# Scaling attention values straight out of PSUM on VectorE in a fused attention and SwiGLU kernel

## The chip, the cores and the metric

The kernel runs on one core of a Trainium2 chip. A core has TensorE (PE in the profile, with its weight loads as PEld), VectorE (DVE), ScalarE (ACT), GpSimd (POOL) and SyncE (SP), which work on their own queues of instructions and wait for one another by semaphores. The metric is the device time of one execution in microseconds (us); lower is better.

## The reference

Attention with a local window of 96 keys and 8 global keys feeds a SwiGLU feed-forward block:

```python
# q, k, v: (4 batches, 8 heads, 768, 64) float32
scores = scale * np.matmul(q, k.transpose(0, 1, 3, 2)) + bias     # bias = -slope * distance
scores = np.where(is_global | is_local, scores, -1e9)
a = np.exp(scores - max)
a = a / (np.sum(a, axis=-1, keepdims=True) + 1e-09)
x = np.matmul(a, v)                  # to (3072 tokens, 512)
g = x @ w_gate                       # w_gate, w_val: (512, 1536)
out = (g * sigmoid(g) * (x @ w_val)) @ w_out                      # w_out: (1536, 512)
```

The kernel does the division last: it sums the unnormalized weights (the denominators, `den`) and the weighted values (the numerators, `num`), and multiplies `num` by the inverted `den`. Inputs are float32; the products are taken in float16 and summed in float32.

## The kernel before

The 3072 tokens are eight tiles of 384. A tile is half a batch (`half` 0 or 1). Attention is worked in pairs of heads (`Pair`) and quads of heads (`Quad`, two per batch, `g` 0 or 1). TensorE is kept busy by mixing attention steps of one batch into the feed-forward groups of the batch before.

PSUM has eight banks. Four, `a0` to `a3`, go round for the attention steps; three, `x0` to `x2`, go round for gate and value products; `o0` holds output sums:

```python
    state = {"tags": ["a0", "a1", "a2", "a3"], "n": 0, "x": ["x0", "x1", "x2"]}

    def bank(name, dt=FP32):
        tag = state["tags"][state["n"] % len(state["tags"])]
        state["n"] += 1
        return single(name, tag, dt)

    def banks(name, dt=FP32):
        return [bank(name, dt) for _ in range(2)]
```

A bank is written again only after the last reader of what it held before. A scores step takes two banks (one per head of the pair), a values step three. Work for the other engines can be put in the list `later`, from which one entry is issued ahead of each group of matmuls:

```python
    def run_later(n):
        for _ in range(n):
            if later:
                later.pop(0)()
    # class Quad (cut)
        def invert(self, den):
            dT = sb2.tile([128, TB], FP32, name="dT", tag="dT")
            self.dR = sb2.tile([128, TB // 32], FP32, name="dR", tag="dR")
            nc.vector.transpose(dT, den[:, 0:TB])
            nc.vector.reciprocal(
                out=self.dR, in_=dT.rearrange("p (n i) -> p n i", i=32)[:, :, 0])

        def spread(self):
            self.rb = sb2.tile([128, TB], FP32, name="rb", tag="rb")
            nc.vector.transpose(
                self.rb.rearrange("p (n i) -> p n i", i=32),
                self.dR.unsqueeze(2).broadcast_to([128, TB // 32, 32]))

        def values(self, half, bank, mul_eng):
            den = bank("den")
            self.weigh(half, den, None)
            srcs = []
            for side in range(2):
                num = bank("num")
                self.weigh(half, num, side)
                src = sb2.tile([128, TB], FP32, name="ns", tag="ns")
                nc.scalar.copy(out=src, in_=num[:, 0:TB])
                srcs.append(src)

            def scale_num(side):
                mul_eng.tensor_mul(self.x_out(half, side), srcs[side], self.rb)
            ... (cut: invert, spread and the products go into `later`)
```

`weigh` is the run of matmuls; `mul_eng` is VectorE for batch 0 and GpSimd for the others. With GpSimd, both products are issued together with `spread`; with VectorE they are two entries of their own. The feed-forward group takes tanh on ScalarE (`th`) and two operations on VectorE (`sl`, `hT`):

```python
    def gate_or_val(t, f, which, c0=0):
        products(t, f, which, c0, NC)          # four matmuls into one of x0, x1, x2
        dst = gv.pop((f, which))
        if which == 0:
            ...
            nc.scalar.activation(out=th, in_=dst[:, 0:TB], func=AF.Tanh, scale=0.5)
            nc.vector.scalar_tensor_tensor(
                out=sl, in0=th, scalar=1.0, in1=dst[:, 0:TB], op0=AluOp.add, op1=AluOp.mult)
            gv["sl"] = sl
        else:
            nc.vector.tensor_mul(hTs[t][:, f, :], dst[:, 0:TB], gv["sl"])
```

The attention steps come in lists, each inner list being one step of the loop below. `sc` and `sch` are scores, `va` is values (batch, g, half), `tr` and `trh` transposes, `fetch` transposes by DMA, `sp` puts `spread_keys` (three VectorE copies into `kT`, L407, L410, L411) into `later`:

```python
    def first(b):
        return [[tr(b, 0), tr(b, 1)],
                [sc(b, 0, 0), sc(b, 0, 1)], [sc(b, 1, 0), sc(b, 1, 1), fetch(b, 2, 3)],
                [sp(b, 2), va(b, 0, 0), sp(b, 3)],
                [sc(b, 2, 0), sc(b, 2, 1)],
                [sc(b, 3, 0), sc(b, 3, 1)], [va(b, 1, 0)]]

    def both(b):
        n = b + 1
        return [[sc(b, 0, 2), sc(b, 1, 2)], [sc(b, 2, 2), sc(b, 3, 2), fetch(n, 0, 1)],
                [va(b, 0, 1)], [sp(n, 0), va(b, 1, 1), sp(n, 1)],
                [sc(n, 0, 0), sc(n, 0, 1), fetch(n, 2, 3)], [sp(n, 2), sc(n, 1, 0), sc(n, 1, 1)],
                [va(n, 0, 0), sp(n, 3)], [sc(n, 2, 0), sc(n, 2, 1)],
                [sc(n, 3, 0), sc(n, 3, 1)], [va(n, 1, 0)]]

    half1 = [[trh(0)], [trh(1)], [sch(0, 0), sch(0, 1)], [trh(2)], [sch(1, 0), sch(1, 1)],
             [trh(3)], [va(0, 0, 1)], [sch(2, 0), sch(2, 1)],
             [sch(3, 0), sch(3, 1)], [va(0, 1, 1)]]
    stretches = [
        (ff(0, 0, 10), half1),
        (ff(0, 10, 12) + ff(1, 0, 3), []),
        (ff(1, 3, 12, (1, 1, 2)), fst),                      # fst = first(1)
        (ff(2, 0, 12, (1,)) + ff(3, 0, 12, (1,)), both(1)),
        (ff(4, 0, 12, (1,)) + ff(5, 0, 12, (1,)), both(2)),
        (ff(6, 0, 12, (1,)), second(3)),
        (ff(7, 0, 12, (1,)), [])]
    ... (cut)
        work = sum(g[0] for g in groups)
        quota = len(steps) / (work - (1.0, 0, 6.0, 6.0, 6.0, 6, 3.0)[n])
        owed = -0.1 if n == 0 else 0.4
        for w, t, f, which in groups:      # gate, val, and output parts where there are any
            ... (cut: loads; at a tile's first group all of `later` is issued)
            run_later(1)
            if which == 2:
                out_part(*outs.pop(0))
            else:
                gate_or_val(t, f, which, NC if t == 0 and f < 2 else 0)
            owed += w * quota
            while owed >= 1.0 and steps:
                run_later(len(later))
                for step in steps.pop(0):
                    step()
                owed -= 1.0
```

So a step that comes due first issues all that is still in `later`. Half 0 of batch 0 is done ahead of these loops by `denominators` and `numerators`, which multiply out of PSUM on VectorE.

Of the kernel before, what the change touches and what calls it, by code (L numbers as in the profile page):

```python
# [9 lines left out]
FP32 = mybir.dt.float32  # L10
# [27 lines left out]
def kernel(  # L38
# [12 lines left out]
    nc = tc.nc  # L51
# [13 lines left out]
    TB = 384  # L65
    scale = float(1.0 / np.sqrt(D))
# [24 lines left out]
    sb2 = ctx.enter_context(tc.tile_pool(name="sb2", bufs=2))  # L91
# [16 lines left out]
    for hp in range(2):  # L108
        for st, src in ((k32, k), (q32, q)):
            nc.sync.dma_start(  # L110
                out=st[:, 2 * hp:2 * hp + 2, :],
                in_=src[0, 2 * hp:2 * hp + 2, 0:TB, :].rearrange(
                    "h (p j) d -> p h (j d)", p=128))
# [29 lines left out]
    for j in range(J2):  # L143
        nc.vector.tensor_copy(
            out=perm[:, j, :, NG + j::J2],
            in_=identx.rearrange("p (c m) -> p c m", c=NC0))
        n = (NG - j + J2 - 1) // J2
        nc.vector.tensor_copy(
            out=perm[:, j, :, j:NG:J2],
            in_=identx[:, 0:n].unsqueeze(1).broadcast_to([128, NC0, n]))  # L150
# [85 lines left out]
# [4 lines that stand above are left out]
# [12 lines left out]
    later = []  # L252
# [163 lines left out]
    class Quad:  # L416
# [46 lines left out]
        def x_out(self, half, side):  # L463
            return x_of(2 * self.b + half)[:, 2 * self.g + side, :]

        def values(self, half, bank, mul_eng):
            den = bank("den")
            self.weigh(half, den, None)
            srcs = []
            for side in range(2):  # L470
                num = bank("num")
                self.weigh(half, num, side)
                src = sb2.tile([128, TB], FP32, name="ns", tag="ns")
                nc.scalar.copy(out=src, in_=num[:, 0:TB])  # L474
                srcs.append(src)

            def scale_num(side):
                mul_eng.tensor_mul(self.x_out(half, side), srcs[side], self.rb)  # L478

            def spread():  # L480
                self.spread()
                if mul_eng is nc.gpsimd:
                    for side in range(2):
                        scale_num(side)

            later.append(lambda: self.invert(den))
            later.append(spread)
            if mul_eng is not nc.gpsimd:
                for side in range(2):
                    later.append(lambda side=side: scale_num(side))  # L490

        def denominators(self, den):
            self.weigh(0, den, None)
# [2 lines left out]

        def numerators(self, side, num):
            self.weigh(0, num, side)
            nc.vector.tensor_mul(self.x_out(0, side), num[:, 0:TB], self.rb)


    hTs = {}
# [62 lines left out]
    quads = {(b, g): Quad(b, g) for b in range(B) for g in range(2)}  # L565
# [104 lines left out]
        return lambda: pairs[b, hp].scores(bk, nc.vector if on_vector else nc.gpsimd, bool(later))  # L670

    def va(b, g, half):
        return lambda: quads[b, g].values(half, bank, nc.vector if b == 0 else nc.gpsimd)

    def tr(b, hp):
        return pairs[b, hp].transposes
# [12 lines left out]
    def second(b):  # L689
        return [[sc(b, 0, 2), sc(b, 1, 2)], [sc(b, 2, 2), sc(b, 3, 2)],  # L690
                [va(b, 0, 1)], [va(b, 1, 1)]]
# [7 lines left out]
# [6 lines that stand above are left out]
# [131 lines left out]
```

The softmax here doesn't subtract the row's maximum and nothing guards it: scores larger than these inputs give would overflow.

## Time and profile before

| | |
|---|---|
| time, median of 3 | 253.78 us (253.47 to 254.28) |
| span of the profiled execution | 252.9 us |
| granted TensorE clock, mean | 0.998 |
| GpSimd products, L478 | 24, 23.9 us busy |
| ScalarE copies, L474 | 28, 12.0 us busy |
| tanh on ScalarE, L527 | 94, 46.4 us busy |
| VectorE sl, L529, and hT, L533 | 94 each, 51.8 and 51.7 us busy |

A group line of the profile names the source line, the engine, the operation, the output and inputs by the program's names, the shapes and the count, and then the busy time. A timeline line has start, length, engine, line and what it does; overlapping instructions of one kind are merged with a count (x2), so that two products of 0.55 us can show as one piece of 1.01. In brackets is the idle time before it on that engine, and what ended it. Busy times of one engine can overlap a little, and matmul ends are modelled.

### The profile page before, as it was taken

What the parts mean: (1) busy time and instruction counts of PE and PEld (TensorE: products, weight loads), DVE (VectorE), ACT (ScalarE), POOL (GpSimd) and SP (SyncE); (2) the same over time, 40 slices, a digit from 0 to 9 for tenths busy, and PEclk for the clock granted to TensorE, in tenths of its full rate; (3) what the DMA queues carried; (4) which work ended last, traced back from release to release, by engine and by line L of the source; (5) the groups of instructions that cost most, each with busy time, mean ns of one, the idle gap of its engine ahead of it and who ended that gap; (6) DMA issues with size and microseconds to landing.
All of it is one profiled execution on the core that took longest, in us unless ns stands there. A gap on an engine that the chain in (4) does not pass through costs nothing.

```text
span 252.9 us, 5999 instructions
## 1 busy us (share of the span) xinstructions
PE 241.3 (95%) x2384; PEld 136.1 (54%) x2384; DVE 168.7 (67%) x379; ACT 130.9 (52%) x290; POOL 105.0 (42%) x123
## 2 busy tenths in 40 slices
PE   6997999899889999999999999999999999999994
PEld 4664556464435556555555555555555555555541
DVE  7365779856695666979785656978875666555510
ACT  3476787559464455464653653555735634332321
POOL 9663664550054975913609865803020232200000
PEclk9999999999999999999999999999999999999999
DMA  6999999991950999993916997991011101100122
GB/s 157 188 203 181 180 207 205 167 131 42 127 69 4 141 150 173 129 143 64 117 44 67 150 157 88 147 109 45 0 44 41 44 0 44 43 20 24 41 83 83
DMA packets 86499, 25.63 MB, mean 101 GB/s; under 512 B 76288, under 2 KB 83528, under 8 KB 86472
## 3 DMA queue, kind: packets, MB, share of 16 engines
q0 software_dynamic: 65408, 13.83, 65.7%
q1 hardware_dynamic: 20920, 11.30, 21.8%
q8 instruction: 18, 0.29, 0.5%
q10 hardware_dynamic: 144, 0.13, 0.2%
q14 instruction: 9, 0.07, 0.1%
HBM read 28.63 MB, written 6.29 MB: 138 GB/s over the span
## 4 chain that ended last, share of the span: by engine, by line
PE 80%; DVE 8%; ACT 4%; DMA 3%; SPq 2%; issue 1%; DVEq 0%; ACTq 0%
PE ops L545 23%; PE gps L516 22%; PE vps L516 22%; PE num L443 3%; PE sc L366 2%; PE den L443 2%; DVE sl L529 2%; DMA kN<-kst 2%; DMA q<-in_q_dram 2%; ACT at L351 1%; PE trs L296 1%; PE warm L574 1%; PE sc L343 1%; PE psv L598 1%; SPq L399 1%
## 5 line engine op out<-in xcount | busy, mean ns | idle before, releaser
L529 DVE SCALAR_TENSOR_TENSOR sl<-th,gps 128x384 f32<-128x384 f32 x94 | 51.8, 552 | 45.4 <-ACT th L527 44.3
L527 ACT ACTIVATE th<-gps 128x384 f32<-128x384 f32 x94 | 46.4, 494 | 63.1 <-PE gps L516 61.6
L516 PE MATMUL gps<-xT,wg 128*128 128x384 f16 x376 | 77.0, 326 | 0.7 <-DVE xT L478 0.6
L516 PE MATMUL vps<-xT,wv 128*128 128x384 f16 x376 | 76.5, 326 | 0.5 <-DVE sl L529 0.4
L545 PE MATMUL ops<-wo,hT 128*128 128x512 f16 x288 | 75.5, 379 | 0.0
L533 DVE TENSOR_TENSOR hT<-vps,sl 128x384 f16<-128x384 f32 x94 | 51.7, 550 | 7.2
L478 POOL TENSOR_TENSOR xT<-ns,rb 128x384 f16<-128x384 f32 x24 | 23.9, 1013 | 77.5 <-DVE rb L459 62.4
L516 PEld LDWEIGHTS <-wg 128*128 128x128 f16 x384 | 35.8, 98 | 33.1 <-issue 3.1
L516 PEld LDWEIGHTS <-wv 128*128 128x128 f16 x384 | 36.8, 98 | 26.4 <-issue 2.1
L545 PEld LDWEIGHTS <-hT 128*128 128x128 f16 x288 | 27.4, 98 | 25.1 <-issue 0.4
L375 ACT ACTIVATE at<-sc 128x432 f16<-128x432 f32 x72 | 33.6, 535 | 9.0 <-PE sc L366 9.0
L171 POOL DMA_DIRECT2D vS<-in_v_dram x25 | 22.3, 898 | 9.1 <-DMA k<-in_k_dram 3.4
L559 ACT ACTIVATE osb<-ops 128x512 f32<-128x512 f32 x23 | 13.7, 597 | 18.0 <-PE ops L545 18.0
L474 ACT COPY ns<-num 128x384 f32<-128x384 f32 x28 | 12.0, 482 | 12.7 <-PE num L443 11.9
L203 POOL DMA_DIRECT2D qst<-in_q_dram x20 | 16.8, 854 | 2.7 <-DMA wo<-in_moe_w_out_dram 1.6
L203 POOL DMA_DIRECT2D kst<-in_k_dram x20 | 17.0, 865 | 2.0 <-DMA wo<-in_moe_w_out_dram 1.1
L386 DVE TENSOR_TENSOR at<-at,masks 128x864 f16<-128x864 f16 x20 | 12.9, 645 | 4.4 <-ACT at L375 4.4
L351 ACT ACTIVATE at<-sc 128x432 f16<-128x432 f32 (+2 forms) x32 | 11.5, 447 | 5.1 <-PE sc L343 5.1
L386 POOL TENSOR_TENSOR at<-at,masks 128x864 f16<-128x864 f16 x4 | 7.3, 1821 | 13.6 <-ACT at L375 13.6
L443 PE MATMUL num<-at,vS 128*32 128x216 f16 (+6 forms) x560 | 12.0, 226 | 0.0
L443 PE MATMUL den<-at,ones 128*32 128x216 f16 (+6 forms) x288 | 9.4, 229 | 2.4 <-DVE at L383 1.8
L443 PEld LDWEIGHTS <-ones 128*32 128x32 f16 x288 | 5.7, 96 | 9.2 <-issue 8.9
(76 smaller groups left out, 176.1 us busy)
## 6 DMA issues: line engine op xcount, KB each, us to landing
out_dram<-osb SPq DMA_DIRECT2D x23, 256.0 KB, 2.0
vS<-in_v_dram POOLq DMA_DIRECT2D x21, 120.0 KB, 8.1
kst<-in_k_dram POOLq DMA_DIRECT2D x20, 96.0 KB, 4.9
qst<-in_q_dram POOLq DMA_DIRECT2D x20, 96.0 KB, 4.7
wg<-in_moe_w_gate_dram POOLq DMA_DIRECT2D x6, 256.0 KB, 8.6
wv<-in_moe_w_val_dram POOLq DMA_DIRECT2D x6, 256.0 KB, 9.6
wo<-in_moe_w_out_dram POOLq DMA_DIRECT2D x3, 512.0 KB, 11.1
k<-in_k_dram SPq DMA_DIRECT2D x2, 192.0 KB, 3.8
```

The costliest lines, as they stand in the source:

```text
L171: nc.gpsimd.dma_start(out=vSs[b][NG:NG + n, c, :, :], in_=v[b, :, KC * c:KC * c + n, :].rearrange("h p d -> p h d"))
L203: nc.gpsimd.dma_start(out=rows_of(st, b, h // 2)[:, :, h % 2, :], in_=src[b, h].rearrange("(t p) d -> p t d", p=128))
L351: nc.scalar.activation(out=at[:, hi, 0:col + n], in_=sc[hi][:, 0:col + n], func=AF.Exp, scale=scale)
L375: nc.scalar.activation(out=at[:, hi, :], in_=sc[hi][:, 0:BANK], func=AF.Exp, scale=scale)
L386: mul_eng.tensor_mul(at, at, m[:, :, o:o + BANK])
L443: nc.tensor.matmul(dst[r, o:o + n], lhsT=ones[:, 0:32] if side is None else vals[:, 4 * g + j, side::2], rhs=pairs[b, 2 * g + j // 2].at[c ...
L478: mul_eng.tensor_mul(self.x_out(half, side), srcs[side], self.rb)
L516: nc.tensor.matmul(gv[f, which][:, 0:TB], lhsT=w[:, c, 128 * f:128 * f + 128], rhs=x_of(t)[:, c, :], start=(c == 0), stop=(c == NC - 1))
L527: nc.scalar.activation(out=th, in_=dst[:, 0:TB], func=AF.Tanh, scale=0.5)
L529: nc.vector.scalar_tensor_tensor(out=sl, in0=th, scalar=1.0, in1=dst[:, 0:TB], op0=AluOp.add, op1=AluOp.mult)
L533: nc.vector.tensor_mul(hTs[t][:, f, :], dst[:, 0:TB], gv["sl"])
L545: nc.tensor.matmul(ops, lhsT=hTs[t][:, f, 128 * i:128 * i + 128], rhs=wo[:, f, :], start=(f == 0), stop=(f == NFF - 1))
```

## The change

The values of all batches are multiplied by the inverted denominators on VectorE, reading the numerators out of PSUM. The copy to SBUF on ScalarE and the product on GpSimd go. The aim is to drop a step between the matmul and the finished values and to use one path for all batches; ScalarE and GpSimd have less to do, and the bank of a numerator is read by its product itself.

```diff
-        def values(self, half, bank, mul_eng):
+        def values(self, half, bank):
             den = bank("den")
             self.weigh(half, den, None)
-            srcs = []
+            later.append(lambda: self.invert(den))
+            later.append(self.spread)
             for side in range(2):
                 num = bank("num")
                 self.weigh(half, num, side)
-                src = sb2.tile([128, TB], FP32, name="ns", tag="ns")
-                nc.scalar.copy(out=src, in_=num[:, 0:TB])
-                srcs.append(src)
-
-            def scale_num(side):
-                mul_eng.tensor_mul(self.x_out(half, side), srcs[side], self.rb)
-
-            def spread():
-                self.spread()
-                if mul_eng is nc.gpsimd:
-                    for side in range(2):
-                        scale_num(side)
-
-            later.append(lambda: self.invert(den))
-            later.append(spread)
-            if mul_eng is not nc.gpsimd:
-                for side in range(2):
-                    later.append(lambda side=side: scale_num(side))
+                later.append(lambda side=side, num=num: self.scale(half, side, num))
+
+        def scale(self, half, side, num):
+            nc.vector.tensor_mul(self.x_out(half, side), num[:, 0:TB], self.rb)
 ...
         def numerators(self, side, num):
             self.weigh(0, num, side)
-            nc.vector.tensor_mul(self.x_out(0, side), num[:, 0:TB], self.rb)
+            self.scale(0, side, num)
 ...
     def va(b, g, half):
-        return lambda: quads[b, g].values(half, bank, nc.vector if b == 0 else nc.gpsimd)
+        return lambda: quads[b, g].values(half, bank)
```

## The prediction

> **What bounds the kernel now.** I read the busy shares first, then what TensorE (PE) waited for, then the group lines of the instructions that the change touches, then the timeline around two of its places.
>
> ```profile
> PE 241.3 (95%) x2384; PEld 136.1 (54%) x2384; DVE 168.7 (67%) x379; ACT 130.9 (52%) x290; POOL 105.0 (42%) x123
> ```
>
> PE is busy 95% of the span, and the stretch table (20 us each) shows 20.00 of 20 in five of the stretches between 80 and 220 us. VectorE (DVE) has a third of its time free, though up to 16.7 of 20 us are used between 160 and 180. So the end is set by the order of matmuls on PE; another engine counts only where PE stands still for it. Those waits are few. The list of PE's waits (total us, times, longest us):
>
> ```profile
> PE den L443 <- DVE at L383: 1.8, 2, 1.1
> ...
> PE vps L516 <- DVE sl L529: 0.4, 1, 0.4
> ```
>
> All of PE's waits on DVE after the first 25 us come to about 3 us (the two shown, 0.6 for xT at L478, 0.2 for dT). That is all that a relief of DVE, ACT and GpSimd (POOL) could give back.
>
> The instructions concerned, from the lists by tile (least/median/most ns):
>
> ```profile
> L478 POOL TENSOR_TENSOR xT<-ns,rb x24: 988/997/1144, 69.3 to 215.6; 128x384 f16<-128x384 f32 x24
> L499 DVE TENSOR_TENSOR xT<-num,rb x4: 544/547/557, 18.2 to 22.7; 128x384 f16<-128x384 f32 x4
> L478 DVE TENSOR_TENSOR xT<-ns,rb x4: 539/546/548, 40.6 to 48.0; 128x384 f16<-128x384 f32 x4
> ```
> ```profile
> L474 ACT COPY ns<-num x28: 479/482/486, 37.6 to 212.9; 128x384 f32<-128x384 f32 x28
> ```
>
> The L499 line is already the instruction that the change uses everywhere: PSUM times rb. It costs 547 ns on DVE, the same as the SBUF form's 546, and POOL takes 997.
>
> **What the Trainium skill says.** "VectorE: DVE Perf Modes", section on the perf-mode tier table: tensor_tensor runs in its slowest mode both with fp32 in SBUF and with any PSUM input. The trace agrees: 547 against 546 ns. "GPSIMD Engine Reference", Engine selection: two-input elementwise work is about twice as slow there as on VectorE; here 997/546 = 1.8. "SBUF — State Buffer", Who interferes with whom: a VectorE copy in a two-port mode, or a VectorE op with two SBUF inputs beside a GpSimd read, blocks against GpSimd for a whole instruction. The trace agrees at 69 us, shown below. "Perfetto Trace Analysis", Optimizing Tensor Performance, Matmuls: independent groups should rotate through different PSUM banks so that emptying one lies beside the next group's matmuls. This is the point on which my prediction turns: the change makes a bank's emptying late.
>
> **The change part by part.** *Removed from ACT*: 28 copies x 0.482 = 13.5 us, none of which ended a PE wait. *Removed from POOL*: 24 x 0.997 = 23.9 us, off PE's path also. *Added to DVE*: 24 x 0.547 = 13.1 us; the 4 products of batch 0 were on DVE already and only change their source. *Taken back on DVE*: copies and masks that ran beside a POOL product were stretched. L410 has mean 491 ns over 10 against 170 undisturbed (3.2 us), L411 288 against 170 (1.2), L407 413 against 345 (0.7), L386 645 against 600 over 20 (0.9): 6.0 us at most, since POOL's own DMA issues stretch some of these too. DVE's net load rises by 7 to 13 us, most of it between 60 and 220 us, where the stretch table leaves it 45 us idle.
>
> *Moved, and this decides*: when a num bank comes free. Before, ACT emptied it at once after the matmuls. After, it is held until DVE has done invert (dT 0.57, dR 0.23), spread (rb 0.57) and its scale (0.55), each put off by one group of matmuls in the deferred list. Four banks a0..a3 go round. A values step takes k (den), k+1, k+2 (num). If a pair of scores steps comes next, the first takes k+3 and k (den), the second k+1 and k+2: both nums. PE runs in program order, so if the scales aren't done it stands. I counted the groups from each of the 14 values steps to the next use of its num banks by walking the step lists with their quotas. In 12 there are six or more groups of about 0.65 us, enough for the four deferred pieces, or a values step follows whose nums take the old den and the first old num. Two are tight: batch 0, group 0, half 1 (two groups in between) and batch 1, group 0, half 0 (three).
>
> *Place 1*, from the timeline at 39 us:
>
> ```profile
> 39.39 0.48 PE L343 MATMUL sc<-qT,kT 64*128 64x72 f16 x10
> 39.63 0.57 DVE L459 STREAM_TRANSPOSE rb<-dR 128x384 f32<-128x384 f32 x1
> ...
> 40.12 0.52 DVE L529 SCALAR_TENSOR_TENSOR sl<-th,gps 128x384 f32<-128x384 f32 x1
> ...
> 40.56 1.01 DVE L478 TENSOR_TENSOR xT<-ns,rb 128x384 f16<-128x384 f32 x2
> ```
>
> The ten score matmuls are both scores steps; the last six use the num banks and start about 39.55. In the changed kernel they wait for the two scales, which stand in the DVE queue where the L478 pair stands now and end at 41.57. PE goes on with the next vps at about 41.85 in place of 39.80: +2.0 us. It isn't regained nearby: after it the exps on ACT, the mask and the next denominators each wait for the one before, and DVE, which ran almost without a gap from 38 to 45 us, gets a pause of 2 us in which it has nothing to do. The xT wait at 48.6 moves along. I carry all 2.0.
>
> *Place 2*, from the timeline at 68 us:
>
> ```profile
> 68.02 0.53 PE L366 MATMUL sc<-qT,kT 64*128 64x216 f16 x7 [0.17 <-DVE dT L453]
> ...
> 68.56 0.57 DVE L459 STREAM_TRANSPOSE rb<-dR 128x384 f32<-128x384 f32 x1
> ...
> 69.28 2.12 POOL L478 TENSOR_TENSOR xT<-ns,rb 128x384 f16<-128x384 f32 x2 [15.11 <-ACT at L375]
> ...
> 69.48 0.98 DVE L410 COPY kT<-kN 128x48 f16<-128x48 f16 x1
> ...
> 70.46 1.40 DVE L386 TENSOR_TENSOR at<-at,masks 128x864 f16<-128x864 f16 x1
> ```
>
> The first matmul shows the same bank rule already at work: it waits 0.17 us for dT, the reader of den. The last four of the seven use the nums. After rb (end 69.13) come two scales of 0.55, so the nums are free at 69.7 and 70.25, and the next gps starts near 70.55 in place of 68.48: +2.0. Here some comes back. L410 and L386 no longer meet a POOL product, 0.98 to 0.17 and 1.40 to 0.60, so DVE, with two scales more (1.1), is 0.3 to 0.5 us earlier at the end of the mask (71.5 against 71.86), and PE's wait for L383 at 75.56 (1.05 us) can take up part. Worked through to it: gps 70.55, tanh 71.9, the second exps 72.85 (before 70.7), the last exps 76.2, first half of the last mask 76.9, where before it was 75.5. I carry +1.4.
>
> *The other twelve.* The step with spread_keys around it (batches 1 and 2, group 1, half 1) is closest. At 103.74 rb ends; then scale, sl, scale to 105.39, and the bank for the second scores step opens at about 105.45, where the matmul could have gone at 105.1. But there PE waits 0.38 us for sl today, because L410 took 0.97 beside POOL. The one replaces the other: +0.1. In the same step of batch 2, at 158.85 where rb ends, PE has no such wait today, and the bank opens at 160.55 in place of a start near 160.15: +0.4. In the steady stretches the product pushes the next sl by up to 0.6 us; PE needs that bank 0.67 us after sl's end (sl ends at 219.75, the next vps is at 220.42). No stall, small margin.
>
> Sum: 253.8 + 2.0 + 1.4 + 0.5 = 257.7. I take off 0.4 for slack that I may have overlooked: 257.3.
>
> **The rivals.** *DVE becomes the bound.* If the 13.1 us were all on the path the time would be 267; if only in the two fullest stretches, 100 to 120 and 160 to 180 (16.4 and 16.7 us busy of 20, with two values steps or 2.2 us more), one or two us more than mine, 258 to 259. Against it: DVE's idle time before sl is 45 us, waiting for tanh, and most of it lies beside a full PE. For it: the margin of 0.67.
>
> *The relief wins.* ACT is freed of 13.5 us, POOL of 23.9, its queue of loads no longer stands behind products that wait for rb (62 us of such idling), and the port blocking is gone. If the banks came free in time after all, the gain is bounded by the waits on DVE: 0.4 for sl, and about 1 us of the den wait: 252.4. For it: each xT would come 1 to 1.5 us earlier, as a pair on POOL takes 2.0. Against it: only one xT wait exists (0.6 us), in batch 0, where DVE had the product before.
>
> *Only nothing happens.* The loads and copies were all hidden; then 253.8. Against it: the two bank counts leave no room for it.
>
> **Range and chances.** Each place may lose 1 to 2.2 us, and margins elsewhere may cost up to 2 or give 1 back. That is 254.6 to 259.4. The 2% line is at 258.9, reached if both stalls are carried whole and the DVE rival adds a little: 0.17. Faster by 2% would need 248.7, more than all the waits on DVE: 0.01. Within 2%: 0.82.
>
> **What would show it.** Right: PE waits on DVE xT from score matmuls (L343 at about 40 us, L366 at about 70), about 1 to 2 us each and at no other place; L410 near 0.2 us, L386 at 0.60; the scale at 0.55 from PSUM; POOL busy near 81 us, ACT near 117; the delay against before stepping to 2 us at 42 and 3 or more by 77, then flat. Wrong: no such waits (my bank count would be off), a delay that grows steadily from 80 to 220 us with PE waiting for sl or hT (the DVE rival), or PE's gap at 75 taking up all of place 2.

## The result and the profile after

The change makes the kernel slower: 262.57 us (median of 4 runs, 261.54 to 263.38) against 253.74; the ratio is 1.034 with a 95% interval of 1.030 to 1.039. The profiled span grew from 252.9 to 260.2 us. The busy shares of the changed kernel, in the page's first part:

```profile
PE 242.0 (93%) x2384; PEld 135.9 (52%) x2384; DVE 173.6 (67%) x403; ACT 119.2 (46%) x262; POOL 81.1 (31%) x99
```

TensorE (PE) has the same work, ScalarE (ACT) is relieved of 11.7 us and GpSimd (POOL) of 23.9, and VectorE (DVE) is busy only 4.9 us longer although 24 products were added. PE simply stands still longer. What it waits for, changed kernel (total us, times, longest us):

```profile
PE sc L366 <- DMA qT<-qst: 5.8, 2, 5.4
PE sc L343 <- DVE xT L477: 1.7, 2, 1.5
...
PE den L443 <- DVE at L383: 1.2, 2, 0.7
```

The second line is the foreseen bank wait at place 1. The first is a wait that the kernel before doesn't have at all: scores wait for the transposed queries `qT` of batch 1, which a DMA transpose brings. The timeline of the changed kernel at place 1:

```profile
38.40 0.29 PE L343 MATMUL sc<-qT,kT 64*128 64x72 f16 x4
...
39.58 1.01 DVE L477 TENSOR_TENSOR xT<-num,rb 128x384 f16<-128x384 f32 x2
...
40.18 0.26 PE L343 MATMUL sc<-qT,kT 64*128 64x216 f16 x1 [1.49 <-DVE xT L477]
```

Ten score matmuls in a row before are now four, a pause until the first of the two products is done, and the rest. At place 2 the picture is another one:

```profile
64.73 1.34 SPq L399 DMA_TRANSPOSE qT<-qst  x1
...
67.91 0.81 PE L532 MATMUL ops<-wo,hT 128*128 128x512 f16 x3
...
70.18 0.35 DVE L407 COPY kT<-kN 128x720 f16<-128x720 f16 x1 [4.38 <-DMA kN<-kst]
...
72.83 1.02 DVE L477 TENSOR_TENSOR xT<-num,rb 128x384 f16<-128x384 f32 x2
74.12 0.90 PE L366 MATMUL sc<-qT,kT 64*128 64x216 f16 x8 [5.40 <-DMA qT<-qst]
...
74.96 1.46 PE L503 MATMUL gps<-xT,wg 128*128 128x384 f16 x4
76.21 1.47 PE L503 MATMUL vps<-xT,wv 128*128 128x384 f16 x4
```

The scores of one pair of heads wait for the transpose that SyncE issued at 64.73, and start at 74.12. The two products end at 73.85, so the bank wait alone would have held PE nearly as long, but they too are late because of a transpose: VectorE stood 4.38 us for the keys `kN`, and the inversion, rb and the products stand behind that copy in its queue. The next two groups start 1.25 us apart where 0.65 is usual: the granted clock was 0.76 from 72 to 76 us. The Trainium skill ("TensorE: Matmul & The Clock Gate", Part 1) says that the clock halves after some 3.4 us of idling and takes as long to return; a wait of 5.4 us followed by groups at half speed for about 3.4 us, from 74.12 to 77.49, agrees. A shorter wait is followed by the same in a run below, so the 3.4 us of idling are no safe limit here.

Why is the transpose late? Here is GpSimd's queue, first in the kernel before, then in the changed one:

```profile
51.59 1.65 POOL L203 DMA_DIRECT2D qst<-in_q_dram  x2
53.21 0.95 POOL L171 DMA_DIRECT2D vS<-in_v_dram  x1
...
79.09 1.96 POOL L478 TENSOR_TENSOR xT<-ns,rb 128x384 f16<-128x384 f32 x2 [6.12 <-DVE rb L459]
81.00 1.72 POOL L203 DMA_DIRECT2D kst<-in_k_dram  x2
```
```profile
51.70 1.65 POOL L203 DMA_DIRECT2D qst<-in_q_dram  x2
53.33 2.50 POOL L171 DMA_DIRECT2D vS<-in_v_dram  x3
55.80 1.71 POOL L203 DMA_DIRECT2D kst<-in_k_dram  x2
57.45 1.70 POOL L203 DMA_DIRECT2D qst<-in_q_dram  x2
```

Before, GpSimd stood in front of its first product from about 54 to 69 us, and for another 6.12 us in front of a later one, and everything behind them in program order stood too. The rows of batch 2 (`kst`, `qst`) were issued at 81.0. Without products nothing stops the queue, and they go out at 55.8. Four transposes of batch 1, keys and queries of pairs 2 and 3, are issued by SyncE from 62 to 68 us in both kernels. From issue to landing, 60 to 80 us, before and then after (count, KB if known, median us):

```profile
kN<-kst SPq DMA_TRANSPOSE x2, 3.6
qT<-qst SPq DMA_TRANSPOSE x2, 2.8
```
```profile
kN<-kst SPq DMA_TRANSPOSE x2, 9.1
qT<-qst SPq DMA_TRANSPOSE x2, 9.3
```

The chain of waits of the changed kernel runs through the last of them, the qT of pair 3, without anything else for 11 us. It lands at 79.24, and the scores of that pair start at 79.37, after the second and shorter wait of the list:

```profile
68.27 10.97 DMA qT<-qst
```

### The profile page after: what moved, and what is told of

Read it like the earlier page. It is cut to its first block, busy times and chain, and to the rows that moved or that the text cites. A ratio compares the mean times of both kernels' runs of the same rounds, so it can differ in the third digit from the quotient of the medians.

```text
span 260.2 us, 5931 instructions
## 1 busy us (share of the span) xinstructions
PE 242.0 (93%) x2384; PEld 135.9 (52%) x2384; DVE 173.6 (67%) x403; ACT 119.2 (46%) x262; POOL 81.1 (31%) x99
## 4 chain that ended last, share of the span: by engine, by line
PE 76%; DVE 9%; DMA 7%; ACT 4%; issue 1%; SPq 1%; POOL 1%; DVEq 0%; ACTq 0%; POOLq 0%
PE ops L532 22%; PE gps L503 21%; PE vps L503 20%; DMA qT<-qst 4%; PE sc L366 3%; DMA v<-in_v_dram 3%; PE num L443 3%; DVE sl L516 2%; PE den L443 2%; DVE xT L477 2%; ACT at L351 2%; DVE hT L520 2%; PE psv L585 1%; PE sc L343 1%; DVE rb L459 1%
## 5 line engine op out<-in xcount | busy, mean ns | idle before, releaser
L386 POOL TENSOR_TENSOR at<-at,masks 128x864 f16<-128x864 f16 x4 | 7.3, 1818 | 104.8 <-ACT at L375 104.8
L477 DVE TENSOR_TENSOR xT<-num,rb 128x384 f16<-128x384 f32 x32 | 17.0, 549 | 0.3
L366 PE MATMUL sc<-qT,kT 64*128 64x216 f16 (+2 forms) x168 | 10.7, 247 | 5.9 <-DMA qT<-qst 5.8
L386 DVE TENSOR_TENSOR at<-at,masks 128x864 f16<-128x864 f16 x20 | 12.1, 606 | 5.4 <-ACT at L375 5.4
L351 ACT ACTIVATE at<-sc 128x432 f16<-128x432 f32 (+2 forms) x32 | 11.7, 444 | 5.8 <-PE sc L343 5.8
L366 PEld LDWEIGHTS <-kT 64*128 64x128 f16 x168 | 6.2, 95 | 13.1 <-DVE xT L477 6.5
```

Of the source, the lines that this page charges most:

```text
L366: nc.tensor.matmul(sc[hi][:, col:col + n], lhsT=self.kT[r, 128 * c:128 * c + 128], rhs=self.qT[r, q0:q0 + n], start=True, stop=True)
L386: mul_eng.tensor_mul(at, at, m[:, :, o:o + BANK])
L477: nc.vector.tensor_mul(self.x_out(half, side), num[:, 0:TB], self.rb)
```

## The experiments

Theory A: the time goes to loads that run ahead on GpSimd's queue and meet the transposes (the *load* cause), besides the two bank waits. Theory B: the bank waits and VectorE's added load are all of it. Times are medians, and each ratio is to the kernel before on the same chip (253.6 to 254.1 us).

**Holding GpSimd's queue, nothing else.** On the changed kernel, in `spread`:

```diff
+            if self.b > 0:
+                nc.gpsimd.tensor_copy(out=hold, in_=self.rb[:, 0:1])
```

> The changed kernel plus one tiny GpSimd copy (128x1) of rb in each spread of batches 1 to 3, so that GpSimd's queue of loads waits for rb as it did before, without the products. If loads that run ahead and meet the DMA transposes cost the time (theory A): the qT wait of 5.4 us goes and the time falls by 5 to 6 us, to 256 to 257.5; place 2 may then show its bank wait of 1 to 2 us. If late banks and more work on VectorE cost it (theory B): no change, 261 to 263.

Measured: 258.41 us, ratio 1.018 (1.014 to 1.022). One element per partition, read by GpSimd at the right moment, takes 4.2 us off the changed kernel. Its queue and, below, PE's waits:

```profile
71.11 0.18 POOL L463 COPY hold<-rb 128x1 f32<-128x1 f32 x1 [17.04 <-DVE rb L459]
71.34 1.57 POOL L171 DMA_DIRECT2D vS<-in_v_dram  x2
```
```profile
PE sc L343 <- DVE xT L479: 1.7, 2, 1.5
PE sc L366 <- DVE xT L479: 1.6, 2, 1.4
```

The wait for qT is gone, and now place 2 shows a bank wait of its own. The time fell, but it is 0.9 us over what I had written for theory A.

**The load cause alone.** On the kernel before, all products on VectorE, still from the copy in SBUF:

```diff
-        return lambda: quads[b, g].values(half, bank, nc.vector if b == 0 else nc.gpsimd)
+        return lambda: quads[b, g].values(half, bank, nc.vector)
```

> The kernel before with all products on VectorE, still out of the ScalarE copy in SBUF: banks come free early as before, VectorE has the 13 us more, and GpSimd's loads are not held back by products. Theory A: the qT wait near 70 us is there and the time is 259 to 262. Theory B with the banks as cause: 253 to 254.5. If VectorE's load itself is the cause: 256 or more, with waits for sl or hT spread over the run.

Measured: 260.37 us, ratio 1.022 (1.016 to 1.028). Banks come free as early as ever here, and after the start PE has one new wait, for a transpose:

```profile
PE sc L366 <- DMA qT<-qst: 5.1, 1, 5.1
```

So the banks aren't needed for the loss: only the engine that multiplies was changed, and 6.5 us are lost. 5.1 of them are the wait. After it the clock is low: from the gps group behind the wait to the next scores it is 4.79 us (73.12 to 77.91) against 2.70 before (68.48 to 71.18). The edit also gives VectorE 13 us more to do. PE has no wait for sl or hT that would point to this, and the run after next, with as many products on VectorE, loses nothing.

**Place 1 alone.** On the kernel before, batch 0 multiplied out of PSUM:

```diff
+                if self.b == 0:
+                    srcs.append(num[:, 0:TB])
+                    continue
                 src = sb2.tile([128, TB], FP32, name="ns", tag="ns")
```

> The kernel before with only batch 0 multiplied out of PSUM on VectorE; batches 1 to 3 keep copy and GpSimd product. Both theories: the wait at place 1 (scores for DVE xT near 40 us, 1.7 us) alone, and the time 1.0 to 2.0 us over before, 254.8 to 255.8. If place 1 is taken back later: 253.8.

Measured: 256.04 us against 253.89, ratio 1.0075 (1.0052 to 1.0099), that is +2.1 us by the medians (1.3 to 2.5 by the interval), 0.2 over what I had written. PE has the waits at L343 (1.49 and 0.20 us) and, just behind, one of 0.3 us for the mask at L355. By the time of the whole kernel nothing is taken back later.

**Both causes taken away.** The held queue, and on top of it the ScalarE copy kept in two of the 14 values steps, the products still on VectorE:

```diff
                 self.weigh(half, num, side)
+                if (self.b, self.g, half) in ((0, 0, 1), (1, 0, 0)):
+                    src = sb2.tile([128, TB], FP32, name="ns", tag="ns")
+                    nc.scalar.copy(out=src, in_=num[:, 0:TB])
+                    num = src
```

> As the first of these (changed kernel with the tiny GpSimd copy), and the two tight values steps (batch 0 group 0 half 1, batch 1 group 0 half 0) keep the ScalarE copy, so that their banks come free early; the products are on VectorE. Theory A plus my two places: both causes are gone, 253 to 254.5. Theory B with VectorE's load as cause: 256 or more.

Measured: 253.54 us, ratio 1.000 (0.998 to 1.002). All 28 products on VectorE, 24 of them straight from PSUM, cost nothing beyond the noise of 0.2% (0.5 us) once the two banks and the queue are looked after. Within that, the other twelve values steps and VectorE's load play no part.

**The copies without the hold**, which completes the square (the edit is the last one without the two lines of the first):

> The changed kernel with the ScalarE copy kept in the two tight values steps and nothing that holds GpSimd's loads: banks early, loads running ahead. With the two causes as the runs so far have them, the bank waits near 40 and 70 us are gone, the qT waits stay, and the time is near the version with all copies, 259.5 to 261: less than the 8.8 us of the change by about 2, because the second bank wait lies beneath the wait for qT. If the two causes simply add, 258.0.

Measured: 260.14 us, ratio 1.023 (1.021 to 1.026). The four corners:

| median us | loads held | loads run ahead |
|---|---|---|
| tight banks freed early | 253.54 | 260.14 |
| tight banks held until the product | 258.41 | 262.57 |

Banks alone cost 258.41 - 253.54 = 4.9, loads alone 260.14 - 253.54 = 6.6, both 9.0 and not 11.5. The medians don't all come from one chip; with each taken against its own kernel before, banks cost 4.9, loads 6.4, both 9.2, and the overlap is 2.1 in place of 2.5. It is about what place 2 alone costs (2.0 to 2.4, below), which here lies beneath the wait for qT.

**Which loads, and when.** Two versions of the fourth kernel with the tiny copy in one place only. In the first it stands in the values of batch 1, group 1, half 0:

```diff
-            if self.b > 0:
+            if self.hold:
                 nc.gpsimd.tensor_copy(out=hold, in_=self.rb[:, 0:1])
 ... (cut)
         def values(self, half, bank):
+            self.hold = (self.b, self.g, half) == (1, 1, 0)
```

> The version with the tiny GpSimd copy and two ScalarE copies, with the tiny copy in one place only: values of batch 1, group 1, half 0. This lets the v loads of batch 1 run ahead but holds the q and k rows of batch 2. If the rows of batch 2 are what meets the transposes: 253 to 254.5. If the v loads do as well, or run-ahead in later batches costs too: 255 or more.

Measured: 253.06 us, ratio 0.999 (0.996 to 1.001). The v loads did run ahead, at 52.58, and did no harm; the rows of batch 2 were held:

```profile
52.58 2.51 POOL L171 DMA_DIRECT2D vS<-in_v_dram  x3
77.35 0.18 POOL L464 COPY hold<-rb 128x1 f32<-128x1 f32 x1 [22.27 <-DVE rb L460]
77.86 1.70 POOL L203 DMA_DIRECT2D kst<-in_k_dram  x2 [0.33 <-PE gps L512]
```

In the second it stands one values step earlier, with the same edit and `(1, 0, 0)`:

> The same with the tiny copy only in the values of batch 1, group 0, half 0, ten us earlier, so that the rows of batch 2 start near 70 us when the last transpose of batch 1 has been issued. If only an overlap with the transposes matters: 253 to 255, with PE waiting little for qT. If running ahead costs in other ways (later transposes, the copies into kT beside GpSimd's DMA issues): 256 or more.

Measured: 253.55 us, ratio 1.0015 (0.999 to 1.004). The rows of batch 2 are issued from 71.00 us, ten us ahead of the kernel before, and PE has no wait for qT. Two later transposes of this run, issued at 84.2 and 85.6 us amid the rows, take 7.3 and 9.3 us to land, and PE doesn't wait for them. Running ahead is not the harm in itself; it is harmful in the stretch from about 62 to 71 us, in which four transposes are under way and PE is about to need them. One hold in one place undoes it.

**The slow clock after the wait.** On the changed kernel, 50 matmuls with an unused result ahead of the scores that wait, so that PE isn't idle:

```diff
+            if (self.b, hp, bk) == (1, 2, 0):
+                busy = single("busy", state["x"][gv["n"] % len(state["x"])])
+                for _ in range(50):
+                    nc.tensor.matmul(busy[:, 0:256], lhsT=ones[:, 0:128], rhs=ones[:, 0:256],
+                                     start=True, stop=True)
```

> The changed kernel with 50 idle-time matmuls (128x256, result unused) ahead of the scores of batch 1, pair 2, block 0, so that TensorE has work while it waits for the late qT. If part of the loss is the lower clock after the wait (gps takes 1.25 us for four matmuls there in place of 0.65): gps, vps and ops after the wait are at full speed and the time falls by 1.5 to 2.5 us to 260 to 261. If the wait alone counts: no change or a little slower, 262 to 263.

Measured: 261.89 us, ratio 1.0345 (1.031 to 1.038), the same as the change within the noise, and not the 260 to 261 that I had written for the case that the clock counts. Its timeline on PE:

```profile
68.35 5.62 PE L362 MATMUL busy<-ones 128*128 128x256 f16 x50
73.90 0.54 PE L371 MATMUL sc<-qT,kT 64*128 64x216 f16 x8
74.38 0.82 PE L508 MATMUL gps<-xT,wg 128*128 128x384 f16 x4
...
79.05 0.55 PE L371 MATMUL sc<-qT,kT 64*128 64x216 f16 x8 [1.90 <-DMA qT<-qst]
79.53 0.97 PE L508 MATMUL gps<-xT,wg 128*128 128x384 f16 x4
80.29 1.49 PE L508 MATMUL vps<-xT,wv 128*128 128x384 f16 x4
```

The groups at 74 us do run at full speed, so the idling made them slow in the changed kernel. But PE only arrives sooner at the next pair's scores, whose qT lands near 79 us in both kernels (PE gets on at 79.37 there, at 79.05 here), and the slow clock follows now. In the changed kernel the loss is set by the landing of the last transpose, and the low clock lies hidden before it. That doesn't hold for every run: in the second, PE waits for no later transpose, and the low clock is part of the 6.5 us.

## Why the prediction was wrong, by its steps

**What bounds the kernel: right.** PE's order of matmuls sets the end, and every loss begins at a place where PE stands.

**Cost of the product and load on VectorE: right.** From PSUM it took 549 ns mean over 32. L410 fell from 491 to 207 ns, L411 from 288 to 201, L407 from 413 to 340 and L386 from 645 to 606: 5.2 us given back of the 6.0 at most that I had counted. The durations of all VectorE instructions together grew by 7.4 us, at the low end of the 7 to 13; the page's 4.9 counts overlapping time once. The fourth experiment bounds the net effect of the added VectorE work at 0.2% of the time.

**Place 1: right.** +2.0 predicted; 1.69 us of waits and +2.1 us by the third experiment.

**Place 2: right in kind, the size depends on what it is counted from.** +1.4 predicted: 2.0 lost and 0.6 back through the later wait for L383. In the held kernel PE waits 1.41 and 0.20 us. From the gps group at 65.54 us of the kernel before to the one at 76.52 it is 10.98 us; in the held kernel the same stretch takes 12.31, so +1.3, nearly as predicted. But in the third experiment, where place 2 isn't touched, it takes 10.27. The give-back thus doesn't need place 2, and against that run place 2 costs 2.0 us in the traces and 258.41 - 256.04 = 2.4 by the medians.

**The other twelve: not seen.** I had put 0.5 us on them. With the two places cured the time is that of the kernel before, but 0.5 us is also the width of the noise. No trace has a bank wait at any of them.

**The step that failed** is the one on GpSimd: "24 x 0.997 = 23.9 us, off PE's path also". The products' time was off the path, but their waiting was not idle time to be gained. I had seen it, 62 us before rb and 15.11 us before the product at 69.28, and entered it with the relief: "its queue of loads no longer stands behind products that wait for rb". The runs show the reverse. That waiting kept the rows of batch 2 behind the transposes of batch 1. I looked at what the loads would gain and not at what they would meet. The chain of waits of the kernel before already runs through one of these transposes, so it had no time to spare:

```profile
64.88 4.32 DMA kN<-kst
```

The DMA line in 40 slices, before and after:

```profile
DMA  6999999991950999993916997991011101100122
```
```profile
DMA  7999999999999991451100489940111011101122
```

Slices 10 to 13 of the kernel before, about 57 to 82 us, read 1, 9, 5 and 0. The 9, from 63 to 69.5 us, holds the four transposes, which had the engines nearly to themselves. After, all four slices read 9. Of the 9.0 us the load cause, alone or on top of the banks, is 4.2 to 6.6 us, and the range that I gave had no term for it. With it my sum of 257.7 would have been some 262 to 264, an estimate after the fact.

**What stays open.** That the rows delay the transposes is shown by holding them; whether through the share of the sixteen DMA engines, the many small packets (26,597 under 512 B from 50 to 80 us against 11,854), or the order within the engines wasn't tried. Nor was it tried apart what the late kN, for which VectorE waits, adds to the late qT.

## What to carry to other kernels

An instruction that waits in a queue also holds everything behind it; before taking it away, list what stands behind it in program order, when it will start instead, and which urgent transfer is then under way. Where such a brake is useful it can be had cheaply, by a tiny instruction with the same wait (0.18 us here, 0.57 in one run). And before a consumer of a rotating PSUM bank is put off, count the groups to the bank's next use at every place: here 2 of 14 were tight, and the other 12 showed no wait.

## What the runs showed of the hardware

DMA transposes of one pair of heads, issued between 62 and 68 us, took 2.8 to 4.3 us to land in the kernel before and 7.1 to 11.1 us amid the row loads of the changed one. A wait of 5.4 us on PE left the matmuls after it at about half speed for some 3.4 us (granted clock 0.76 and 0.81 in the two stretches from 72 to 80 us); in the kernel with the idle-time matmuls, a wait of 1.90 us was followed by a granted clock of 0.57 from 80 to 84 us, while after waits of 1.4 us in the held kernel the clock stayed at 1.00. Beside GpSimd's product at 69.28 us a VectorE copy of 48 elements took 0.98 us where 0.17 is usual, and without products the mean of those copies was 207 ns.
